# A transformer block on one core: state of the first head group taken one period later, two input chunks on a second DMA queue, startup statistics shared by ScalarE and VectorE

## The chip, the core and the metric

The kernel runs on one core of a Trainium2 chip. A time is device microseconds (us) of one execution. Each quoted time is the median of some executions, with their number and extremes where these matter. The profile of an execution counts from its first to its last instruction; this span is 2.0 to 2.15 us shorter than the time in every run of this study.

Engine names in the profile: PE is TensorE's matmul, PEld its weight load, DVE is VectorE, ACT is ScalarE, POOL is GpSimd, SP is SyncE. SPq and ACTq are DMA issues on the queues of SyncE and ScalarE. Tile names: xch is a chunk of x as loaded, lno the chunk with its mean taken off, xnT its transpose, diag the diagonal matrices of 1/std, e the probabilities, ps any PSUM buffer, and junk the unused output of a ScalarE pass that only sums.

## The reference

One block with a segment-recurrent attention and a gated MLP. What matters here is the attention with its memory (shapes: x is 2048 x 1024, 32 heads of 32, four segments of 512 tokens):

```python
x = A_x
h = x + _A_ref(_layernorm(x), A_wq, A_wk, A_wv, A_wo, A_beta)      # attention with memory
h2 = h + _B_ref(_layernorm(h), B_w_in, B_w_sp, B_b_sp, B_w_out)    # gated MLP
# in _A_ref, for each segment s:
#   p = softmax(q k^T * scale + mask); a_dot = p v
#   o = g * (phi(q) M) / (phi(q) z) + (1 - g) * a_dot
#   M = M + phi(k)^T v ;  z = z + sum phi(k)                       # the "state"
```

The state of a segment is read first in the next segment.

## The kernel before

The kernel records its operations engine by engine; the order of the program text is the order on each engine, and the waits follow from the data. Tokens are worked on in chunks of 128 (x0 to x3 are the four chunks of the first segment), heads in eight groups of four, so a segment has eight periods. The parts that the change touches:

```python
# loads at the start, all issued by SyncE: x0, x1, wv piece, x2, wv piece, x3, wv, wv, wk, ...
for k in range(8):
    if k in (0, 1, 3, 5):
        x_load((k + 1) // 2)
    else:
        i = {2: 0, 4: 2, 6: 4, 7: 6}[k]
        sp.dma_start(WV[0][:, i:i + 2, :], ...)
sp.dma_start(WK[:, :, 0:256], ...)
# ... cut ...
# startup of segment 0: mean of each chunk, centred chunk transposed on PE, 1/std applied later
warm(9)                                            # nine matmuls on dummy data
act_mean(1)                                        # ScalarE: sum of chunk 1
var0(ln_stats(XCH[0]))                             # VectorE: two statistics and their aggregate
c0 = center(0, MV[0][:, 0:1], ALU.subtract)
c1 = center(1, MEAN[1][:])
pe_Th(0, c0, dve, dve)                             # transposes of chunk 0, copies by VectorE
pe_Th(1, c1, act, dve)
# ... cut: chunks 2 and 3, v projections ...
diag(0); ... diag(3)                               # 1/std of the chunks as diagonal matrices (VectorE)
for i in range(2):                                 # and broadcast to all partitions by matmul
    pe.matmul(bank(br), ONES[:], DIAG[i][:]..., start=(i == 0), stop=(i == 1))
# ... cut ...
sp.dma_start(WK[:, :, 256:D], wcols(A_wk, 256, D))   # 1.5 MB
sp.dma_start(WQ[:, :, 256:D], wcols(A_wq, 256, D))   # 1.5 MB
phi_exp(0)
phi_max(0)                                         # ends with the DMA transpose pk <- pqk
```

In period n PE works on the logits of group n and on pv of group n-1, followed by the state of group n-1, which needs pk, a DMA transpose of phi(k):

```python
def pv(n, cqs=range(4)):
    ...                                            # probabilities times v
    if 3 in cqs:
        state(n)                                   # four matmuls ps <- v,pk
        norm(n)                                    # VectorE; calls state_sum(n): PSUM -> msum, then GpSimd
```

The softmax here doesn't subtract the row's maximum and nothing guards it: scores larger than these inputs give would overflow.

Of the kernel before, what the change touches and what calls it, by code (L numbers as in the profile page):

```python
# [6 lines left out]
F32 = mybir.dt.float32  # L7
I32 = mybir.dt.int32
ACTF = mybir.ActivationFunctionType
ALU = mybir.AluOpType  # L10

T = 2048
D = 1024
# [6 lines left out]
NQ = 8  # L20
# [237 lines left out]
def bass_sequential_preLN__memory_aug_infini_attn__mixer_gmlp__prompt_kernel(  # L258
# [14 lines left out]
    x2d = A_x[0]  # L273
    out2d = out[0]
    R = _Recorder(nc)
    pe, act, dve, pool, sp = R.pe, R.act, R.dve, R.pool, R.sp
# [6 lines left out]
    def tens(name, shape, dt, off):  # L283
        sz = int(np.prod(shape[1:])) * mybir.dt.size(dt)
        assert off % 32 == 0 and off + sz <= ARENA, (name, off, sz)
        t = nc.alloc_sbuf_tensor_at(name, list(shape), dt, offset=abase + off)
        R.space[t[:].tensor.name] = ("sbuf", off)
        return t
# [13 lines left out]
    cb = Bump(0, 14 * K)  # L302
# [5 lines left out]
    BLK = cb("blk", [128, 4], F32)  # L308
    dead = cb.c
    MASKG = cb("maskg", [128, NQ, 4, 33], F32)  # L310
    MSUM = cb("msum", [128, NQ, 132], F32)
    MZB = cb("mzb", [128, NQ, 48], BF16)
    UPD = [cb("upd%d" % i, [128, 132], F32) for i in range(2)]
    DGM = cb("dgm", [128, 4, 33], F32)
    HALF2 = cb("half2", [128, 2, 33], F32)
    MHALF = cb("mhalf", [128, 1], F32)
    STATS = [cb("stats%d" % i, [128, 2, 6], F32) for i in range(4)]
    MV = [cb("mv%d" % i, [128, 2], F32) for i in range(4)]
# [9 lines left out]
    WV = [tens("wv%d" % i, [128, 8, 512], BF16, (46 + 8 * i) * K) for i in range(2)]  # L328
# [3 lines left out]
    b1 = Bump(110 * K, 134 * K)  # L332
# [5 lines left out]
    b1 = Bump(110 * K, 120 * K)  # L338
    ONES = b1("ones", [128, 128], BF16)
    MEAN = [b1("mean%d" % i, [128, 1], F32) for i in range(4)]  # L340
    RB = b1("rb", [128, L], F32)
    DIAG = [b1("diag%d" % i, [128, 4, 128], BF16) for i in range(2)]
    JUNK = b1("junk", [128, D], BF16)
    b2 = Bump(134 * K, ARENA)
    ZSTG = [tens("zstg%d" % i, [128, 448], F32, (134 + 2 * i) * K) for i in range(4)]
    XCH = [b2("xch%d" % i, [128, D], BF16) for i in range(4)]
# [3 lines left out]
    PK = [b2("pk%d" % i, [128, 4, 128], BF16) for i in range(3)]  # L350
# [3 lines left out]
    V = b2("v", [128, 4, H, 34], BF16)  # L354
# [17 lines left out]
    PS = nc.alloc_psum_tensor("ps", [128, 8, 512], F32)  # L372
    R.space[PS[:, 0, :].tensor.name] = ("psum", 0)

    def bank(b):
        return PS[:, b, :]

    PVX = PS[:, 4:6, :].rearrange("p b w -> p (b w)")[:, 0:688].rearrange("p (q w) -> p q w", w=172)
    PVA = PVX[:, :, 0:132].rearrange("p q (i w) -> p q i w", w=33)
    STB = PS[:, 5, 176:308]  # L380

    rot = {"banks": list(range(8)), "n": 0}

# [7 lines left out]
            pe.matmul(dst, lhs(i), rhs(i), start=(i == 0), stop=(i == n - 1))  # L391


    def x_load(tc):
        sp.dma_start(XCH[tc % 4][:], x2d[tc * 128:(tc + 1) * 128, :])

    def wcols(ap, lo, hi):
        return ap[:, lo:hi].rearrange("(c p) n -> p c n", p=128)

    for k in range(8):  # L400
        if k in (0, 1, 3, 5):
            x_load((k + 1) // 2)
        else:
            i = {2: 0, 4: 2, 6: 4, 7: 6}[k]
            sp.dma_start(WV[0][:, i:i + 2, :],
                         A_wv[i * 128:(i + 2) * 128, 0:512].rearrange("(c p) n -> p c n", p=128))
    sp.dma_start(WK[:, :, 0:256], wcols(A_wk, 0, 256))
    sp.dma_start(BETAB[:], A_beta.partition_broadcast(128))
    sp.dma_start(WQ[:, :, 0:256], wcols(A_wq, 0, 256))
# [3 lines left out]
    pool.memset(MHALF[:], -0.5)  # L413
    dve.memset(ETMP[:], 0.0)
    act.activation(RDM[:, 0, 0:1], MHALF[:], ACTF.Exp)
    pool.iota(IOT[:], [[1, 128]], base=0, channel_multiplier=-1)
    pool.memset(V[:, :, :, 32:34], 1.0)
    pool.memset(BLK[:], 1.0)
# [23 lines left out]
    def ln_stats(src):  # L442
        k = lnc[0] % 4
        lnc[0] += 1
        for i in range(2):
            dve.bn_stats(STATS[k][:, i, :], src[:, i * 512:(i + 1) * 512])
        dve.bn_aggr(MV[k][:], STATS[k][:])
        return k
# [13 lines left out]
    def to_T(dst, tcl, src):  # L462
        sp.dma_start_transpose(dst[:, :, tcl * 128:(tcl + 1) * 128], src[:])
# [24 lines left out]
    def v_mm(s, tcl, half, b, i):  # L488
        pe.matmul(bank(b), XNT[s % 2][:, i, tcl * 128:(tcl + 1) * 128], WV[half][:, i, :],
                  start=(i == 0), stop=(i == 7))  # L490
# [15 lines left out]
    def qk_out(n, which, b):  # L506
        if n < NQ:
            dve.tensor_tensor(QK[n % 2][:, which, :], bank(b), RB[:], ALU.mult)
        else:
# [50 lines left out]
    def pv(n, cqs=range(4)):  # L560
        c = n % NQ
        for cq in cqs:
            for j in range(cq + 1):
                rnd, o = {0: (0, cq * 128), 1: (1, cq * 128 - 128), 2: (2, cq * 128 - 256), 3: (1, 384)}[j]
                for i in range(4):
                    pe.matmul(PVA[:, cq, i, :], E[n % 2][rnd][:, i, o:o + 128], V[:, j, 4 * c + i, 0:33],
                              start=(cq % 3 == 0 and j == 0 and i == 0), stop=False, skip_group_check=True)
        if 3 in cqs:
            state(n)
            norm(n)  # L570

    def mem(n):
# [14 lines left out]
    def norm(n):  # L587
        s, c = divmod(n, NQ)
        ot = OTOK[s % 2][:, :, c * 128:(c + 1) * 128].rearrange("p q (i d) -> p q i d", d=32)
        dve.reciprocal(RD[:], PVA[:, :, :, 32])  # L590
        dve.tensor_tensor(RD[:], RD[:], OMG[:, c:c + 1, :].to_broadcast([128, 4, 4]), ALU.mult)
        rb = RD[:].unsqueeze(3).to_broadcast([128, 4, 4, 32])
        if s == 0:
            dve.tensor_tensor(ot, PVA[:, :, :, 0:32], rb, ALU.mult)
        else:
            dve.tensor_tensor(TA[:], PVA[:, :, :, 0:32], rb, ALU.mult)
        state_sum(n)
        if s > 0:
            dve.tensor_tensor(ot, TA[:], TM[n % 2][:], ALU.add)
        if c == NQ - 1:  # L600
            for tcl in range(4):
                to_T(OT, tcl, OTOK[s % 2][:, tcl, :])

    def state(n):
        s, c = divmod(n, NQ)
        for tcl in range(4 if s < NSEG - 1 else 0):
            pe.matmul(STB, PK[n % 3][:, tcl, :], V[:, tcl, 4 * c:4 * c + 4, 0:33], start=(tcl == 0), stop=(tcl == 3))

    def state_sum(n):
        s, c = divmod(n, NQ)  # L610
        if s == NSEG - 1:
            return
        if s == 0:
            dve.tensor_copy(MSUM[:, c, :], STB)
        else:
            dve.tensor_copy(UPD[n % 2][:], STB)
            pool.tensor_tensor(MSUM[:, c, :], MSUM[:, c, :], UPD[n % 2][:], ALU.add)
        pool.tensor_tensor(DGM[:], MSUM[:, c, :].rearrange("p (i d) -> p i d", d=33), MASKG[:, c, :, :], ALU.mult)
        pool.tensor_tensor(HALF2[:], DGM[:, 0:2, :], DGM[:, 2:4, :], ALU.add)
        pool.tensor_tensor(MZB[:, c, 0:33], HALF2[:, 0, :], HALF2[:, 1, :], ALU.add)  # L620

# [34 lines left out]
    def warm(k):  # L656
        for _ in range(k):
            pe.matmul(bank(7), IDENT[:], ETMP[:, 0, :], start=True, stop=True)

    def center(tc, mean, op=ALU.add):  # L660
        o = LNO[tc % 3]
        dve.tensor_single_scalar(o[:], XCH[tc][:], mean, op)
        return o

    def act_mean(tc):
        act.activation(JUNK[:], XCH[tc][:], ACTF.Copy, scale=-1.0 / D, accum_out=MEAN[tc][:])

    def act_var(tc):
        act.activation(JUNK[:], XCH[tc][:], ACTF.Square, bias=MEAN[tc][:], accum_out=RS[tc][:, 1:2])
        pool.tensor_scalar(RS[tc][:, 0:1], RS[tc][:, 1:2], 1.0 / D, float(LN_EPS), ALU.mult, ALU.add)  # L670

    def var0(k):
        pool.tensor_single_scalar(RS[k][:, 0:1], MV[k][:, 1:2], float(LN_EPS), ALU.add)

    def rstd0(tc):
        pool.tensor_tensor(RS0[tc][:], RS[tc][:, 0:1], MHALF[:], ALU.pow)

    def diag(tc):
        dve.tensor_single_scalar(DIAG[0][:, tc, :], IDENT[:], RS0[tc][:], ALU.mult)
        dve.scalar_tensor_tensor(DIAG[1][:, tc, :], IDENT[:], RS0[tc][:], DIAG[0][:, tc, :], ALU.mult, ALU.subtract)  # L680

    def pe_Th(tcl, src, e0, e1):
        pe_T(XNT[0], tcl, src, (e0, e1))

    warm(9)
    act_mean(1)
    var0(ln_stats(XCH[0]))
    c0 = center(0, MV[0][:, 0:1], ALU.subtract)
    c1 = center(1, MEAN[1][:])
    pe_Th(0, c0, dve, dve)  # L690
    pe_Th(1, c1, act, dve)
    act_mean(2)
    rstd0(0)
    var0(ln_stats(XCH[1]))
    rstd0(1)
    c2 = center(2, MEAN[2][:])
    act_mean(3)
    vb = [next_bank() for _ in range(2)]
    for i in range(4):
        for t in range(2):  # L700
            v_mm(0, t, 0, vb[t], i)
    pe_Th(2, c2, act, dve)
    c3 = center(3, MEAN[3][:])
    for i in range(4, 8):
        for t in range(2):
            v_mm(0, t, 0, vb[t], i)
    var0(ln_stats(XCH[2]))
    rstd0(2)
    pe_Th(3, c3, act, dve)
    act_var(3)  # L710
    rstd0(3)
    diag(0)
    v_out(0, 0, 0, vb[0])
    diag(1)
# [8 lines left out]
    for i in range(2):  # L723
        pe.matmul(bank(br), ONES[:], DIAG[i][:].rearrange("p c n -> p (c n)"), start=(i == 0), stop=(i == 1))
    act.activation(RB[:], bank(br), ACTF.Copy)
    qk_out(0, 1, bk)
# [48 lines left out]
    for n in range(LAST + 1):  # L775
        s, c = divmod(n, NQ)
# [116 lines left out]
    for tb in range(4):  # L893
# [9 lines left out]
        for tcl in range(4):  # L903
            tc = 4 * tb + tcl
# [38 lines left out]
```

## Time and profile before

The time before was 796.97 us (three executions, 796.62 to 797.53). The profiled execution took 797.42 us.

The first two parts of the profile page say that TensorE is busy almost all the time (busy us, share of the span, instructions):

```profile
span 795.4 us, 13019 instructions
## 1 busy us (share of the span) xinstructions
PE 784.7 (99%) x5565; PEld 378.3 (48%) x5657; DVE 380.0 (48%) x745; ACT 295.6 (37%) x347; POOL 173.8 (22%) x329
```

The waits view for PE of the kernel before gives its idle time by cause (us in total, times, longest us); the whole execution has only six such entries, 3.6 us together, and they all lie in the first 31 us:

```profile
PE ps L209 <- DVE ident L209: 1.7, 1, 1.7
PE ps L209 <- DMA pk<-pqk: 0.8, 1, 0.8
PE ps L209 <- DVE lno L209: 0.5, 2, 0.3
...
```

The timeline of the kernel before shows the startup (start, us, engine, operation, output <- inputs, count, and in brackets the idle time before with what ended it):

```profile
3.70 1.42 DVE L209 BATCH_NORM_STATS2 stats<-xch 128x6 f32<-128x512 bf16 x2 [2.01 <-DMA xch<-in_A_x_dram]
4.31 1.06 ACT L209 ACTIVATE junk<-xch 128x1024 bf16<-128x1024 bf16 x1 [2.02 <-DMA xch<-in_A_x_dram]
5.94 1.07 PE L209 MATMUL ps<-ident,lno 128*128 128x128 bf16 x16 [0.17 <-DVE lno L209]
...
15.18 0.35 DVE L209 SCALAR_TENSOR_TENSOR diag<-ident,rs,diag 128x128 bf16<-128x128 bf16 x1
...
15.53 0.59 PE L209 MATMUL ps<-diag,ones 128*128 128x512 bf16 x2
...
19.51 0.40 PE L209 MATMUL ps<-qk 32*128 32x512 bf16 x4
```

Read it thus: x0 has landed at 3.7 us and x1 at 4.3, PE transposes from 5.94, the last diagonal is ready at 15.53 just as PE arrives, and the first logits come at 19.51. "First logits" is the mark of the startup.

The PE timeline of the kernel before, further on, shows the other wait, and the two marks between which group 1 and group 2 run:

```profile
26.11 0.40 PE L209 MATMUL ps<-qk 32*128 32x512 bf16 x4
...
29.19 0.57 PE L209 MATMUL ps<-v,e 128*128 128x33 bf16 x16
30.52 0.41 PE L209 MATMUL ps<-v,pk 128*128 128x132 bf16 x4 [0.76 <-DMA pk<-pqk]
...
34.64 0.39 PE L209 MATMUL ps<-qk 32*128 32x512 bf16 x4
...
42.25 0.39 PE L209 MATMUL ps<-qk 32*128 32x512 bf16 x4
```

The state matmuls (`ps<-v,pk`) of group 0 wait for pk. The first logits of group 1 stand at 26.11, so group 1's period takes 8.53 us, group 2's 7.61, and every later one 7.60. The chain of waits says where pk was: issued at 19.55, and 10.92 us until it landed, with 3 MB of wk and wq ahead of it in the queue.

```profile
19.55 10.92 DMA pk<-pqk
```

### The profile page before, as it was taken

The numbers are of one execution on the slowest core, as the hardware profiler recorded it, in microseconds if no ns is written. First come the engines' busy times: TensorE is split into PE (matmuls) and PEld (weight loads), VectorE is DVE, ScalarE is ACT, GpSimd is POOL, SyncE is SP. The second block draws the span as 40 slices with busy tenths as digits, with TensorE's granted clock in tenths as the row PEclk, the third lists the DMA queues.
The fourth block names the chain that finished last, engine by engine and source line by source line (L and its number), as shares of the span: only waits on it lengthen the run. The fifth ranks groups of instructions, "written<-read, shape, count | busy, mean of one in ns | idle before, by whom it ended". The sixth has DMA issues, their size and how long they took to land.

```text
span 795.4 us, 13019 instructions
## 1 busy us (share of the span) xinstructions
PE 784.7 (99%) x5565; PEld 378.3 (48%) x5657; DVE 380.0 (48%) x745; ACT 295.6 (37%) x347; POOL 173.8 (22%) x329
## 2 busy tenths in 40 slices
PE   8999999999999999999999999999999999999998
PEld 3445455554554455455544444444444444444444
DVE  7664689679954765744562000053234323323332
ACT  5777877887787675133333333100000000000000
POOL 4554565566553331100230000000000000000000
DMA  9762555353415425411116000640270143021003
GB/s 296 175 160 60 94 81 121 87 103 84 110 22 126 114 65 136 125 47 54 54 54 132 1 1 0 220 92 7 79 133 1 33 108 78 1 59 54 1 7 86
DMA packets 125002, 64.83 MB, mean 82 GB/s; under 512 B 94992, under 2 KB 113936, under 8 KB 124944
## 3 DMA queue, kind: packets, MB, share of 16 engines
q1 hardware_dynamic: 124944, 63.99, 33.7%
q8 instruction: 44, 0.72, 0.4%
q14 instruction: 14, 0.11, 0.1%
HBM read 32.51 MB, written 8.39 MB: 51 GB/s over the span
## 4 chain that ended last, share of the span: by engine, by line
PE 94%; DVE 3%; DMA 2%; issue 1%
PE ps L209 94%; DMA pk<-pqk 1%; DVE stats L209 1%; DMA xch<-in_A_x_dram 0%; DVE hch L209 0%; DVE otok L209 0%; DVE lno L209 0%; DVE pqk L209 0%; DVE ta L209 0%; DVE xnT L209 0%; DVE rd L209 0%; DVE mv L209 0%; DVE etmp L209 0%; DVE rdm L209 0%; DVE upd L209 0%
## 5 line engine op out<-in xcount | busy, mean ns | idle before, releaser
L209 PE MATMUL ps<-wspT,z 128*128 128x512 bf16 x878 | 193.1, 379 | 0.9
L209 ACT ACTIVATE e<-ps 128x2048 bf16<-128x2048 f32 (+1 forms) x96 | 152.7, 1590 | 42.4 <-PE ps L209 42.3
L209 PEld LDWEIGHTS ps<-wspT,z 128*128 128x128 bf16 x896 | 87.7, 98 | 105.7
L209 DVE TENSOR_TENSOR tmpg<-ps,brow 128x512 f32<-128x512 f32 x56 | 38.7, 691 | 196.7 <-DMA brow<-in_B_b_sp_dram 103.7
L209 POOL TENSOR_SCALAR_AFFINE_SELECT e<-e 128x512 bf16<-128x512 bf16 x128 | 90.3, 717 | 126.2 <-ACT e L209 125.9
L209 PE MATMUL ps<-win,hnT 128*128 128x448 bf16 x512 | 98.4, 352 | 0.0
L209 PE MATMUL ps<-w_out,yT 128*128 128x512 bf16 (+2 forms) x453 | 96.9, 372 | 0.5
L209 PE MATMUL ps<-hnT,win 128*128 128x512 bf16 x439 | 96.2, 379 | 0.5
L209 PEld LDWEIGHTS ps<-win,hnT 128*128 128x128 bf16 x512 | 49.7, 98 | 46.4 <-issue 0.2
L209 PEld LDWEIGHTS ps<-w_out,yT 128*128 128x128 bf16 x462 | 44.7, 98 | 52.3
L209 PEld LDWEIGHTS ps<-hnT,win 128*128 128x128 bf16 x448 | 43.8, 98 | 52.8
L209 PE MATMUL ps<-xnT,wk 128*128 128x512 bf16 x234 | 59.6, 380 | 1.2
L209 PE MATMUL ps<-wv,xnT 128*128 128x512 bf16 x255 | 59.2, 380 | 0.3 <-ACT xnT L209 0.2
L209 ACT ACTIVATE z<-ps 128x448 bf16<-128x448 f32 x60 | 32.5, 543 | 69.4 <-PE ps L209 69.4
L209 PE MATMUL ps<-wo,oT 128*128 128x512 bf16 x254 | 57.7, 379 | 0.1
L209 ACT ACTIVATE z1T<-ps 128x512 bf16<-128x512 f32 x56 | 33.4, 597 | 63.3 <-PE ps L209 63.3
L209 DVE TENSOR_TENSOR fin<-fin,ps 128x512 bf16<-128x512 bf16 (+2 forms) x33 | 22.2, 671 | 71.3 <-DMA fin<-out_dram 39.9
L209 PE MATMUL ps<-xnT,wq 128*128 128x512 bf16 x225 | 53.9, 379 | 1.8 <-issue 0.2
L209 DVE BATCH_NORM_STATS2 zst<-z 128x6 f32<-128x448 bf16 x64 | 38.9, 620 | 30.1 <-ACT z L209 30.1
L209 PEld LDWEIGHTS ps<-v,e 128*128 128x128 bf16 x1280 | 38.8, 96 | 14.0 <-issue 6.5
L209 PE MATMUL ps<-v,e 128*128 128x33 bf16 x1280 | 42.2, 178 | 0.0
L209 DVE TENSOR_TENSOR yT<-tmpg,z1T 128x512 bf16<-128x512 f32 x56 | 38.8, 692 | 1.9
(86 smaller groups left out, 611.8 us busy)
## 6 DMA issues: line engine op xcount, KB each, us to landing
xch<-in_A_x_dram SPq DMA_DIRECT2D x16, 256.0 KB, 3.5
xr<-in_A_x_dram SPq DMA_DIRECT2D x16, 256.0 KB, 4.0
out_dram<-hch SPq DMA_DIRECT2D x16, 256.0 KB, 2.4
fin<-out_dram SPq DMA_DIRECT2D x16, 256.0 KB, 2.8
out_dram<-fin SPq DMA_DIRECT2D x31, 128.0 KB, 1.7
win<-in_B_w_in_dram SPq DMA_DIRECT2D x4, 896.0 KB, 5.1
w_out<-in_B_w_out_dram SPq DMA_DIRECT2D x1, 3584.0 KB, 12.8
win<-in_B_w_in_dram SPq DMA_DIRECT2D x3, 1024.0 KB, 5.1
```

The lines of the kernel that those rows point to most:

```text
L209: ins = getattr(e, op.name)(*op.args, **op.kw)
```

## The change

Its intent is to take waits out of the start. The state of group 0 is computed one period later, with that of group 1, when pk has surely landed; x2 and x3 come through ScalarE's own DMA queue, so SyncE issues the rest sooner; chunk 0's mean is summed half by ScalarE and half by VectorE; and the variance of chunk 2 joins that of chunk 3 on ScalarE. Cut to its core:

```diff
-    STB = PS[:, 5, 176:308]
+    STB = [PS[:, 5, o:o + 132] for o in (176, 308)]
@@ loads
-    for k in range(8):  ...  (x0, x1, wv, x2, wv, x3, wv, wv on SyncE)
+    x_load(0)
+    x_load(1)
+    for i in range(0, 8, 2):
+        sp.dma_start(WV[0][:, i:i + 2, :], ...)
@@
     act.activation(RDM[:, 0, 0:1], MHALF[:], ACTF.Exp)
+    x_load(2, act)
+    x_load(3, act)
@@ pv
-            state(n)
+            if n:
+                state(n)
+            if n == 1:
+                state(0)
             norm(n)
@@ norm
-        state_sum(n)
+        if n:
+            state_sum(n)
+        if n == 1:
+            state_sum(0)
@@ startup
+    def act_half(tc):     # ScalarE: -mean of columns 0..511
+        act.activation(JUNK[:, 0:512], XCH[tc][:, 0:512], ACTF.Copy, scale=-1.0 / D, accum_out=MEAN[tc][:])
+    def dve_half(tc):     # VectorE: sum of columns 512..1023, added to it
+        dve.tensor_reduce(out=HSUM[:], in_=XCH[tc][:, 512:D], axis=mybir.AxisListType.X, op=ALU.add)
+        dve.scalar_tensor_tensor(MEAN[tc][:], HSUM[:], -1.0 / D, MEAN[tc][:], ALU.mult, ALU.add)
     warm(9)
+    act_half(0)
+    dve_half(0)
     act_mean(1)
-    var0(ln_stats(XCH[0]))
-    c0 = center(0, MV[0][:, 0:1], ALU.subtract)
+    c0 = center(0, MEAN[0][:])
+    stats0(0, 0)
     c1 = center(1, MEAN[1][:])
-    pe_Th(0, c0, dve, dve)
-    pe_Th(1, c1, act, dve)
+    pe_Th(0, c0, dve, act)
+    pe_Th(1, c1, dve, dve)
@@ ... cut ...
-    var0(ln_stats(XCH[2]))
+    act_var(2)
+    act_var(3)
+    stats0(1, 1)
+    aggr0(1)              # VectorE aggregate, then GpSimd: variance + eps, power -1/2
     rstd0(2)              # GpSimd: power -1/2
-    pe_Th(3, c3, act, dve)
-    act_var(3)
     rstd0(3)
+    pe_Th(3, c3, dve, dve)
     diag(0)
```

More of the change, by code (lines that the diff above doesn't have):

```diff
@@ L310, in bass_sequential_preLN__memory_aug_infini_attn__mixer_gmlp__prompt_kernel @@
     MASKG = cb("maskg", [128, NQ, 4, 33], F32)
-    MSUM = cb("msum", [128, NQ, 132], F32)
+    MSUM = cb("msum", [128, NQ, 136], F32)
     MZB = cb("mzb", [128, NQ, 48], BF16)
@@ L340, in bass_sequential_preLN__memory_aug_infini_attn__mixer_gmlp__prompt_kernel @@
     MEAN = [b1("mean%d" % i, [128, 1], F32) for i in range(4)]
+    HSUM = b1("hsum", [128, 1], F32)
     RB = b1("rb", [128, L], F32)
@@ L391, in mm8, with x_load @@
             pe.matmul(dst, lhs(i), rhs(i), start=(i == 0), stop=(i == n - 1))
-    def x_load(tc):
-        sp.dma_start(XCH[tc % 4][:], x2d[tc * 128:(tc + 1) * 128, :])
+    def x_load(tc, eng=sp):
+        eng.dma_start(XCH[tc % 4][:], x2d[tc * 128:(tc + 1) * 128, :])
     def wcols(ap, lo, hi):
         return ap[:, lo:hi].rearrange("(c p) n -> p c n", p=128)
-    for k in range(8):
-        if k in (0, 1, 3, 5):
-            x_load((k + 1) // 2)
-        else:
-            i = {2: 0, 4: 2, 6: 4, 7: 6}[k]
-            sp.dma_start(WV[0][:, i:i + 2, :],
-                         A_wv[i * 128:(i + 2) * 128, 0:512].rearrange("(c p) n -> p c n", p=128))
+    x_load(0)
+    x_load(1)
+    for i in range(0, 8, 2):
+        sp.dma_start(WV[0][:, i:i + 2, :], A_wv[i * 128:(i + 2) * 128, 0:512].rearrange("(c p) n -> p c n", p=128))
     sp.dma_start(WK[:, :, 0:256], wcols(A_wk, 0, 256))
@@ L606, in state @@
         for tcl in range(4 if s < NSEG - 1 else 0):
-            pe.matmul(STB, PK[n % 3][:, tcl, :], V[:, tcl, 4 * c:4 * c + 4, 0:33], start=(tcl == 0), stop=(tcl == 3))
+            pe.matmul(STB[n == 0], PK[n % 3][:, tcl, :], V[:, tcl, 4 * c:4 * c + 4, 0:33], start=(tcl == 0), stop=(tcl == 3))
     def state_sum(n):
@@ L613, in state_sum @@
         if s == 0:
-            dve.tensor_copy(MSUM[:, c, :], STB)
+            dve.tensor_copy(MSUM[:, c, 0:132], STB[n == 0])
         else:
-            dve.tensor_copy(UPD[n % 2][:], STB)
-            pool.tensor_tensor(MSUM[:, c, :], MSUM[:, c, :], UPD[n % 2][:], ALU.add)
-        pool.tensor_tensor(DGM[:], MSUM[:, c, :].rearrange("p (i d) -> p i d", d=33), MASKG[:, c, :, :], ALU.mult)
+            dve.tensor_copy(UPD[n % 2][:], STB[0])
+            pool.tensor_tensor(MSUM[:, c, 0:132], MSUM[:, c, 0:132], UPD[n % 2][:], ALU.add)
+        pool.tensor_tensor(DGM[:], MSUM[:, c, 0:132].rearrange("p (i d) -> p i d", d=33), MASKG[:, c, :, :], ALU.mult)
         pool.tensor_tensor(HALF2[:], DGM[:, 0:2, :], DGM[:, 2:4, :], ALU.add)
@@ L683, in pe_Th, with stats0, aggr0 @@
         pe_T(XNT[0], tcl, src, (e0, e1))
+    def act_half(tc):
[3 more added lines that the diff above has]
+        dve.scalar_tensor_tensor(MEAN[tc][:], HSUM[:], -1.0 / D, MEAN[tc][:], ALU.mult, ALU.add)
+    def stats0(k, i):
+        dve.bn_stats(STATS[k][:, i, :], XCH[k][:, i * 512:(i + 1) * 512])
+    def aggr0(k):
+        dve.bn_aggr(MV[k][:], STATS[k][:])
+        var0(k)
+        rstd0(k)
     warm(9)
+    act_half(0)
+    dve_half(0)
     act_mean(1)
-    var0(ln_stats(XCH[0]))
-    c0 = center(0, MV[0][:, 0:1], ALU.subtract)
+    c0 = center(0, MEAN[0][:])
+    stats0(0, 0)
     c1 = center(1, MEAN[1][:])
-    pe_Th(0, c0, dve, dve)
-    pe_Th(1, c1, act, dve)
+    pe_Th(0, c0, dve, act)
+    pe_Th(1, c1, dve, dve)
     act_mean(2)
-    rstd0(0)
-    var0(ln_stats(XCH[1]))
-    rstd0(1)
+    stats0(0, 1)
+    aggr0(0)
     c2 = center(2, MEAN[2][:])
@@ L701, in bass_sequential_preLN__memory_aug_infini_attn__mixer_gmlp__prompt_kernel @@
             v_mm(0, t, 0, vb[t], i)
-    pe_Th(2, c2, act, dve)
+    pe_Th(2, c2, dve, act)
     c3 = center(3, MEAN[3][:])
+    stats0(1, 0)
     for i in range(4, 8):
```

## The prediction

> **What bounds the kernel now.** TensorE. Part 1 of the profile page has PE busy 784.7 of 795.4 us; the chain of waits puts 94% of the span on PE. The waits view, for PE alone, adds up to 3.6 us, all in the first 31 us: 1.7 us for the identity at the start, 0.8 us for the first transpose of pk, about 1 us in pieces of 0.2 to 0.3 us. The change can only gain inside that sum, plus what it saves before the first real matmul. From 34 us the timeline shows a group every 7.60 us with no PE wait.
>
> **State of group 0 one period later (the certain part).** PE finishes pv of group 0 at about 29.6 us and starts the four state matmuls only at 30.52, when pk lands (10.9 us after its issue at 19.55, behind 3 MB of wk and wq). In the next group the step takes 0.42 us, here 1.33: 0.91 us go. The four matmuls (0.45 us) only move. The next deadline is the second wq load: it lands at 29.2 us and would be wanted at about 29.6, so it should just not bind. What comes back: in the period with both states DVE does one more copy (0.28 us, about 0.20 after overlap) before the qk copy that ended at 42.10 us, with logits at 42.25: almost no slack. I expect logits of group 3 to wait 0.1 to 0.25 us.
>
> **Startup.** Chunk 0's mean by halves replaces two statistics and an aggregate (1.67 us after landing at 3.68) by about 1.0 us, estimated from half of the 1.06 us ScalarE pass, a reduce near the 0.69 us of a 512-wide statistic, and a 0.2 us combine. But PE is in order and nine warm matmuls, one each 0.43 us, occupy it to about 5.6: first transposes at 5.6 instead of 5.94. Chunk 1's stay near 6.3, but its copies end 0.4 us earlier; chunk 2 transposes at about 8.9 (9.45 before), chunk 3 at 11.1 (11.63). Of loads on a second queue the Trainium skill, "DMA: Bandwidth & Descriptors", section "Issuing engines are not separate DMA queues", says that they run on the same 16 engines and save only issue time. I expect no more total bandwidth: DMA share is near or over 1 from 5 to 28 us.
>
> That half microsecond is mostly lost at the broadcast of the diagonals: ScalarE now runs two variances in a row (1.13 us each) to about 12.4, and GpSimd's in-order queue puts three powers (about 0.64 us each) behind the last. diag 3 ends near 15.4 to 15.8 us (15.53 before), while PE arrives at about 14.9 and waits 0.4 to 0.8 us. First logits at about 19.4 (19.51 before): startup gains 0.0 to 0.3 us.
>
> **Sum.** 0.91 + 0.15 - 0.2 = about 0.85 us. Time 796.1 us; 8 in 10 between 795.3 and 797.0. Faster by over 2%: 0.003; within 2%: 0.994; slower: 0.003.
>
> **What shows each step.** No PE wait for pk; eight state matmuls together after pv of group 1; a new PE wait for diag near 15 us; a small wait for qk before logits of group 3; group 1's period near 7.2 us, group 2's near 8.2. First transposes directly after the warm matmuls. The rest the same, shifted.
>
> **What would make it wrong.** The second wq load landing later, so that PE waits near 29.5 (gain about 0.4); wv pieces delayed by x2 and x3; powers on GpSimd overlapped, so that the startup gain reaches PE in full (gain 1.4).

## The result, and the profile after

The kernel after took 797.39 us (six executions, 797.32 to 797.70), the kernel before in the same rounds 796.79 us (six executions, 796.33 to 797.53). The ratio is 1.0008 with a 95% interval from 0.9995 to 1.0021. The time is the same within the noise, 0.6 us longer by the medians, where 0.85 us less was forecast: outside the forecast's range.

The page of the kernel after looks the same as before; a change of half a microsecond in 795 can't be read from shares. (PE's busy time is higher because fewer matmul records are missing from this trace: 5657 of 5657, against 5565 before.)

```profile
span 795.3 us, 13119 instructions
## 1 busy us (share of the span) xinstructions
PE 790.2 (99%) x5657; PEld 378.5 (48%) x5657; DVE 379.2 (48%) x745; ACT 297.1 (37%) x350; POOL 171.8 (22%) x329
```

The waits view for PE of the kernel after has no wait for pk any more, and a new one for the diagonals:

```profile
PE ps L209 <- DVE ident L209: 1.7, 1, 1.7
PE ps L209 <- DVE lno L209: 0.6, 1, 0.6
PE ps L209 <- DVE diag L209: 0.2, 1, 0.2
...
```

The timeline of the kernel after, at the start:

```profile
0.93 0.86 ACTq L209 DMA_DIRECT2D xch<-in_A_x_dram  x2
...
2.08 0.20 ACT L209 ACTIVATE rdm<-mhalf 128x1 f32<-128x1 f32 x1
...
4.07 0.69 DVE L209 TENSOR_REDUCE hsum<-xch 128x1 f32<-128x512 bf16 x1 [2.39 <-DMA xch<-in_A_x_dram]
...
5.46 1.06 ACT L209 ACTIVATE junk<-xch 128x1024 bf16<-128x1024 bf16 x1 [0.67 <-DMA xch<-in_A_x_dram]
...
5.65 0.98 PE L209 MATMUL ps<-ident,lno 128*128 128x128 bf16 x8
...
7.19 0.62 PE L209 MATMUL ps<-ident,lno 128*128 128x128 bf16 x8 [0.55 <-DVE lno L209]
...
16.04 0.35 DVE L209 SCALAR_TENSOR_TENSOR diag<-ident,rs,diag 128x128 bf16<-128x128 bf16 x1
16.06 0.10 PEld L209 LDWEIGHTS ps<-diag,ones 128*128 128x128 bf16 x1 [0.68 <-DVE diag L209]
...
20.22 0.39 PE L209 MATMUL ps<-qk 32*128 32x512 bf16 x4
```

ScalarE's two loads are issued at 0.93 us, in the midst of SyncE's first two (0.80 and 1.25), although in the program they stand behind an activation that ran at 2.08. x0 is now read from 4.07 instead of 3.70, and x1 from 5.46 instead of 4.31. (A landing in this document is the start of the first reader, where that reader waited for it.) Chunk 0 is transposed from 5.65, directly behind the warm matmuls, as forecast; but chunk 1 only from 7.19, and everything behind it is late. The first logits come at 20.22 instead of 19.51: the startup lost 0.71 us. Most of that shows only at the diagonals: wk starts at 13.98, 0.17 us later than before (13.81), and wq at 16.68, 0.72 us later (15.96). The experiments separate the two: the late loads cost about 0.7 us, the shared statistics win 0.5 us up to wk and lose it again at the diagonals.

The DMA view of the kernel after, from 3 to 5 us, has a second queue (packets, MB, share of the 16 engines). q1 is SyncE's queue; q10 is ScalarE's, since it appears only in runs with loads on ScalarE:

```profile
q10 hardware_dynamic: 225, 0.42, 54.1%
q1 hardware_dynamic: 212, 0.37, 48.3%
```

In these 2 us the second queue moved 0.42 MB and SyncE's, which carries x0 and x1, 0.37 MB; in the kernel before SyncE's queue moved 0.62 MB in the same window.

The PE timeline of the kernel after, further on, has the marks of groups 1 and 2 and the eight state matmuls between them:

```profile
26.82 0.40 PE L209 MATMUL ps<-qk 32*128 32x512 bf16 x4
...
34.19 0.39 PE L209 MATMUL ps<-qk 32*128 32x512 bf16 x4
...
37.68 0.63 PE L209 MATMUL ps<-v,pk 128*128 128x132 bf16 x8
...
42.13 0.39 PE L209 MATMUL ps<-qk 32*128 32x512 bf16 x4
```

With the first logits of group 1 at 26.82, group 1 takes 7.37 us (8.53 before) and group 2 takes 7.94 (7.61): 0.83 us are won over the two. So this pair of traces reads 0.71 lost and 0.83 won, and the spans are 0.1 us apart. That the medians are 0.6 us apart the other way is not in these two traces.

### The profile page after: what moved, and what is told of

The parts are those of the page before. It is cut to its first block, busy times and chain, and to the rows that moved or that the text cites. A ratio compares the mean times of both kernels' runs of the same rounds, so it can differ in the third digit from the quotient of the medians.

```text
span 795.3 us, 13119 instructions
## 1 busy us (share of the span) xinstructions
PE 790.2 (99%) x5657; PEld 378.5 (48%) x5657; DVE 379.2 (48%) x745; ACT 297.1 (37%) x350; POOL 171.8 (22%) x329
## 4 chain that ended last, share of the span: by engine, by line
PE 98%; ACT 1%; DMA 1%; DVE 0%; issue 0%; POOL 0%; SPq 0%; ACTq 0%
PE ps L209 98%; DMA xch<-in_A_x_dram 1%; ACT junk L209 0%; ACT e L209 0%; DVE diag L209 0%; POOL rs L209 0%; ACT xnT L209 0%; DVE lno L209 0%; DVE xnT L209 0%; SPq L209 0%; DVE fin L209 0%; ACTq L208 0%
## 5 line engine op out<-in xcount | busy, mean ns | idle before, releaser
L209 PE MATMUL ps<-xnT,wq 128*128 128x512 bf16 x256 | 60.6, 379 | 0.0
```

The lines of the kernel that those rows point to most:

```text
L209: ins = getattr(e, op.name)(*op.args, **op.kw)
```

## The experiments

Twelve kernels ran, in three lots on one chip each. The runs of the kernel before in a lot serve as its reference: medians 796.94 (lot 1), 796.89 (lot 2) and 796.49 (lot 3), nine executions each. All results were correct. The 95% intervals of the ratios to before are about 0.0013 to either side, 1 us; only that of act_late excludes 1 (1.0026, from 1.0013 to 1.0039). So what follows rests on the traces and on ranges that do not overlap. One trace per run was kept, and identical startups differ: in the five traces that share the startup of before, the first logits stand between 19.26 and 19.61.

| run | lot | median us (five executions) | lowest to highest | first logits in the trace, us |
|---|---|---|---|---|
| before_again | 1 | 797.10 | 796.60 to 798.03 | 19.61 |
| state_only | 1 | 796.62 | 796.52 to 796.79 | 19.43 |
| loads_sp | 1 | 796.66 | 796.35 to 796.85 | 19.54 |
| loads_act | 1 | 797.37 | 797.16 to 797.40 | 20.17 |
| act_late | 2 | 798.95 | 798.81 to 799.41 | 21.75 |
| pow_first | 2 | 796.35 | 796.21 to 796.73 | 19.05 |
| pow_sum4 | 2 | 796.20 | 795.96 to 796.33 | 18.82 |
| pk_ahead | 2 | 797.00 | 796.25 to 797.36 | 19.26 |
| pk_split | 3 | 796.37 | 796.34 to 796.55 | 19.47 |
| pow_sum4_split | 3 | 796.12 | 795.74 to 796.18 | 18.73 |
| pow_pk_split | 3 | 795.85 | 795.75 to 796.30 | 18.79 |
| x3_act | 3 | 796.96 | 796.93 to 797.12 | 19.82 |

### The kernel before, once more

No edit.

> The kernel before, unchanged. It asks two things. First, how much of a time lies outside the span: the kernel after had a span 0.1 us shorter than the one profile of before, and yet a median 0.6 us longer. Theory A (the one profiled execution of before, 797.42 us, was a slow one of its kind): times minus spans are 2.0 to 2.1 us for both kernels, and the spans of before spread from 794.3 to 795.5 with a median near 794.8. Rival B (a second DMA queue costs a fixed time outside the span): spans of before stay near 795.4 and times minus spans come out near 1.4 us. Second, whether the 0.91 us that PE waits for pk is the same in another execution: A expects a shorter wait in faster executions.

Times minus spans are 2.0 to 2.1 us for the kernel before, as for the kernel after and for every variant with the second queue, so rival B is out. The profiled execution of this run took 796.60 us (span 794.5), 0.8 less than the one profiled first. Its PE timeline:

```profile
29.29 0.57 PE L209 MATMUL ps<-v,e 128*128 128x33 bf16 x16
29.70 0.40 PE L209 MATMUL ps<-v,pk 128*128 128x132 bf16 x4
```

The state matmuls follow pv at once: there is no wait for pk at all. pk was issued at 19.7 and took 8.9 us, against 10.9 in the first profile. The wait that the change was sized on is one draw of something that varies; the 14 executions of before and of this copy in lot 1 spread from 796.43 to 798.03.

### The state alone

```diff
 (kernel before, with only the edits of STB, MSUM, pv, norm, state and state_sum shown above)
```

> Only the state of group 0 moves. If the prediction's first part holds by itself: no PE wait for pk, the period of group 1 about 1.1 us shorter and of group 2 about 0.3 us longer, first logits at 19.5 as before, so 0.6 to 0.9 us less than before. If the wait in typical executions of before is shorter than in the profiled one, less: 0.2 to 0.5 us.

The median is 0.32 us under that of before in the same lot, at the lower expectation. What it does is shown by the spread: 0.27 us, against 1.24 us for before (nine executions). The slow executions are gone, but the fastest of before (796.43) is faster than the fastest of this one (796.52). The trace shows why: group 1 takes 7.37 us and group 2 takes 7.95, together 15.32, while the undisturbed execution of before needs 15.21. Without a wait to remove, moving the state costs 0.1 us.

### All loads on SyncE, the rest of the change kept

```diff
 (kernel after)
-    x_load(2, act)
-    x_load(3, act)
 (and the load loop of the kernel before in place of the new one)
```

> The kernel after, with all four chunks of x loaded by SyncE in the order of before. Theory (the second queue's loads of x2 and x3 share the engines with x0 and x1, whose landing came at 4.07 and 5.46 instead of 3.68 and 4.29, and that pushed the whole startup): x1 lands near 4.3, chunk 1 transposes near 6.3 instead of 7.19, diagonals ready near 15.6 instead of 16.4, first logits at 19.3 to 19.6 instead of 20.22, time 0.6 to 0.9 us below the kernel after. Rival (the two variances in a row and the three powers behind them delay the diagonals whatever the loads do): first logits stay at 20.0 or later, time within 0.3 us of the kernel after.

796.66 us, 0.73 us under the kernel after (797.39, measured in other rounds). The timeline of this variant:

```profile
3.56 0.69 DVE L209 TENSOR_REDUCE hsum<-xch 128x1 f32<-128x512 bf16 x1 [2.02 <-DMA xch<-in_A_x_dram]
...
4.31 1.06 ACT L209 ACTIVATE junk<-xch 128x1024 bf16<-128x1024 bf16 x1
```

x0 is there at 3.56 and x1 by 4.31, and the first logits come at 19.54, not 20.22. So the loads are what made the startup late; the slowest of these five executions (796.85) is faster than the fastest of the kernel after (797.32), and than the fastest of loads_act in the same lot (797.16). But the rest of the startup change brings nothing either: this variant is level with the state alone (796.66 and 796.62 in the same lot). Its PE timeline shows the reason, which had been forecast:

```profile
13.30 1.89 PE L209 MATMUL ps<-xnT,wk 128*128 128x512 bf16 x8
15.38 0.78 PE L209 MATMUL ps<-diag,ones 128*128 128x512 bf16 x2 [0.19 <-DVE diag L209]
15.99 1.89 PE L209 MATMUL ps<-xnT,wq 128*128 128x512 bf16 x8
```

PE comes to the diagonals half a microsecond earlier than before (wk starts at 13.30, not 13.81), and then waits for them: wq starts at 15.99, against 15.96 before. The last diagonal is ready at 15.71, inside the 15.4 to 15.8 of the prediction.

### The loads alone

```diff
 (kernel before)
-    (load loop)
+    x_load(0); x_load(1); four wv pieces        # SyncE
     act.activation(RDM[:, 0, 0:1], MHALF[:], ACTF.Exp)
+    x_load(2, act)
+    x_load(3, act)
```

> The kernel before, with only x2 and x3 moved to ScalarE's queue. Theory: x1 lands near 5.4 and x0 near 4.1, first logits 0.3 to 0.7 us later than before. As pk lands behind the same loads, the wait for pk shrinks by as much as the startup grows unless pk moves too, so the end is 0 to 0.4 us later. Rival B of the first run (fixed cost of a second queue outside the span): time minus span grows by 0.5 us or more over that of before.

x0 lands at 4.05, x1 at 5.32, the first logits come at 20.17, 0.6 to 0.7 us later than in the two traces of before; the median is 0.43 us above that of before in the lot. As expected, part of the loss is hidden, since the state would often have waited for pk anyway: this trace has no wait for pk, and the spread is down to 0.24 us. Times minus spans stay at 2.05 to 2.10 us, which is a second answer against a fixed cost of the queue.

### One chunk on the second queue instead of two

```diff
 (loads_sp)
+    if k == 5: continue                         # x3 not on SyncE
     act.activation(RDM[:, 0, 0:1], MHALF[:], ACTF.Exp)
+    x_load(3, act)
```

> The variant with all loads on SyncE (796.66), with x3 alone on ScalarE's queue from its start. Half the dose. Theory (x1 lands late by the bytes that the second queue has in flight before it): x0 lands about 0.4 us late and x1 about 0.5 us late (4.7 to 4.9), first logits 0.2 to 0.5 us later than 19.54, time 796.8 to 797.1. Rival (a second queue has a cost whatever it carries): x1 as late as with both chunks, 5.4, and time near 797.4.

The ScalarE timeline of this variant, where the first pass reads x0 and the second x1:

```profile
0.93 0.38 ACTq L209 DMA_DIRECT2D xch<-in_A_x_dram  x1
...
3.70 0.63 ACT L209 ACTIVATE junk<-xch 128x512 bf16<-128x512 bf16 x1 [1.42 <-DMA xch<-in_A_x_dram]
...
5.05 1.06 ACT L209 ACTIVATE junk<-xch 128x1024 bf16<-128x1024 bf16 x1 [0.62 <-DMA xch<-in_A_x_dram]
```

x1 lands at 5.05: with none, one and two chunks on the second queue it is there by 4.31, 5.05 and 5.46 us, and the first logits come at 19.54, 19.82 and 20.22. The landing with none varies from trace to trace, but stays below the other two: the latest is 4.58, in pow_first. The landing of x1 was somewhat later and that of x0 earlier than expected, the first logits and the time (796.96) are inside. So the cost grows with what the second queue has in flight ahead of x1.

### The second queue's loads issued late

```diff
 (kernel after)
     act.activation(RDM[:, 0, 0:1], MHALF[:], ACTF.Exp)
-    x_load(2, act)
-    x_load(3, act)
@@
     act_half(0)
+    x_load(2, act)
+    x_load(3, act)
```

> The kernel after, with the two loads on ScalarE's queue issued behind its wait for x0 (about 3.6 us) instead of at 0.93 us. Theory (what cost 0.7 us was that x2 and x3 were in flight together with x0 and x1): x0 lands at 3.6 to 3.7 and x1 near 4.3 again, first logits at 19.4 to 19.7, time within 0.2 us of the variant with all loads on SyncE (796.66), though the same queue is used. Rival (loads on a second queue are costly by themselves, by slower landing or by ScalarE's issue time): x2 and x3 land so late, or ScalarE is held up so much, that first logits stay at 20 us or later and the time near 797.4.

Half of the expectation held. The ScalarE timeline of this variant:

```profile
3.45 0.63 ACT L209 ACTIVATE junk<-xch 128x512 bf16<-128x512 bf16 x1 [1.17 <-DMA xch<-in_A_x_dram]
3.46 0.86 ACTq L209 DMA_DIRECT2D xch<-in_A_x_dram  x2
...
9.19 1.06 ACT L209 ACTIVATE junk<-xch 128x1024 bf16<-128x1024 bf16 x1 [2.24 <-DMA xch<-in_A_x_dram]
```

And its PE timeline, at the transposes of chunk 2:

```profile
10.92 0.62 PE L209 MATMUL ps<-ident,lno 128*128 128x128 bf16 x8 [2.16 <-DVE lno L209]
```

x0 and x1 land early again (3.45, and x1 is read from 4.43), so the loads of x2 and x3 had indeed held them up. But x2, issued at 3.46, lands only at 9.2: 5.7 us for 256 KB. The DMA view says where the time went: up to 6.5 us no packet of the second queue moved, while SyncE's queue moved 0.83 MB from 3.46 us on; from 6.5 to 9.2 us the two moved 0.42 and 0.47 MB. Why the first packets came 3 us after the issue, where in the kernel after they came 2 us after it, is not shown. The second queue is not slower for such a load, though: in the kernel before, x3, issued on SyncE at 3.17, landed at 8.76, 5.6 us later as well. PE waits 2.16 us for chunk 2, and the time is 2.1 us above before. My expectation that x2 would still come in time was wrong: these loads are late when issued late, and make others late when issued early.

### The powers ahead of the last variance

```diff
 (loads_sp)
     act_var(2)
-    act_var(3)
+    rstd0(2)
     stats0(1, 1)
     aggr0(1)
-    rstd0(2)
+    act_var(3)
     rstd0(3)
```

> The variant with all loads on SyncE, and on GpSimd the powers of chunks 2 and 1 ahead of the work that waits for ScalarE's second variance. Theory (PE loses about 0.5 us at the diagonals, because three powers, 1.66 us, stand behind the last variance): last diagonal near 15.0 us instead of 15.7, wq at 15.5 instead of 15.99, first logits at 19.0 to 19.15 instead of 19.54, time 0.4 to 0.5 us below that variant, about 796.2. Rival (something else sets the first logits, such as rb or the wq weights): first logits stay within 0.15 us of 19.54.

In the kernel after, GpSimd's queue holds, behind the variance of chunk 3, the three powers. The GpSimd timeline of the kernel after:

```profile
13.36 0.31 POOL L209 TENSOR_SCALAR rs<-rs 128x1 f32<-128x1 f32 x1 [1.08 <-ACT junk L209]
13.73 0.22 POOL L209 TENSOR_SCALAR rs<-mv 128x1 f32<-128x1 f32 x1
14.04 1.66 POOL L209 TENSOR_TENSOR rs<-rs,mhalf 128x1 f32<-128x1 f32 x3
```

In the variant only one power is left behind it, the diagonals are done at 15.11, and PE does not wait for them. Its PE timeline:

```profile
15.07 0.59 PE L209 MATMUL ps<-diag,ones 128*128 128x512 bf16 x2
...
19.05 0.39 PE L209 MATMUL ps<-qk 32*128 32x512 bf16 x4
```

The first logits come at 19.05, as expected and 0.49 us earlier than in loads_sp. The time, 796.35, is 0.31 us under that of loads_sp by the medians (in another lot) where 0.4 to 0.5 was expected. Since startups differ from trace to trace, the stretch from the start of wk to that of wq is the better measure: it takes 2.69 to 2.70 us in after, loads_sp and x3_act, which have the shared statistics and the old order on GpSimd, and 2.15 to 2.16 us in the four variants with the powers first and in the kernel before. So the order on GpSimd was what kept the shared statistics from paying.

### The sum of group 0 where VectorE has time

```diff
 (pow_first)
-        if n == 1:
+        if n == 4:
             state_sum(0)
```

> As the run before it, and the sum of group 0's state is taken on DVE and GpSimd in the period of group 5, where DVE has no statistics of x behind it; its matmuls stay. Theory (the extra copy in the period with both states makes logits of group 3 wait 0.1 us): the period of group 2 is 0.1 us shorter, 7.83 us instead of 7.94, and the time 0.1 us lower, about 796.1. Rival: no such wait, no difference over 0.05 us.

Group 2 takes 7.84 us (32.90 to 40.74) instead of 7.95 in pow_first, so the extra copy did cost 0.1 us of PE. But in this trace group 1 takes 7.48 us instead of 7.37 (wq starts 0.1 us later in it), and the two groups together take 15.32 us as in pow_first: what was won at the copy was lost just ahead of it. The time is 0.15 us lower, 796.20; that this comes from the copy is not shown, since the first logits of the two traces already differ by 0.23 us. Three of its five executions are faster than the fastest of the nine of before in the lot (796.28).

### pk ahead of wq in the queue

```diff
 (kernel before)
-    sp.dma_start(WQ[:, :, 256:D], wcols(A_wq, 256, D))
     phi_exp(0)
     phi_max(0)
+    sp.dma_start(WQ[:, :, 256:D], wcols(A_wq, 256, D))
```

> The kernel before, with only the second wq load issued behind the first transpose of pk instead of ahead of it. Theory (the wait for pk, which differs from one execution to the next, is the queue's: pk lands only after the 3 MB ahead of it): pk lands near 25 to 26 us instead of 28.5 to 30.5, no execution waits for it, and the spread of the times, 1.6 us for before, falls below 0.5 us, with the median at 796.5 or below. The second wq load then lands near 29.7 us and may bind at 30.1. Rival (the spread comes from the landing of x, whatever pk does): the spread stays above 1 us.

pk now lands 5.4 us after its issue and nothing waits for it; but the spread is still 1.11 us and the median that of before. The waits view for PEld (from 15 to 43 us) of this variant has a new entry:

```profile
PEld ps L209 <- DMA wq<-in_A_wq_dram: 0.3, 1, 0.3
```

The wq columns of group 2 are the next deadline, half a microsecond behind that of pk, and the load had been moved behind pk. By itself this run did not decide between the theory and the rival.

### pk ahead, with the loads cut

```diff
 (kernel before)
-    sp.dma_start(WK[:, :, 256:D], wcols(A_wk, 256, D))
-    sp.dma_start(WQ[:, :, 256:D], wcols(A_wq, 256, D))
+    sp.dma_start(WK[:, :, 256:512], wcols(A_wk, 256, 512))
+    sp.dma_start(WQ[:, :, 256:512], wcols(A_wq, 256, 512))
     phi_exp(0)
     phi_max(0)
+    sp.dma_start(WK[:, :, 512:D], wcols(A_wk, 512, D))
+    sp.dma_start(WQ[:, :, 512:D], wcols(A_wq, 512, D))
```

> The kernel before, with the second wk and wq loads cut in two (columns 256 to 511 first) and the first transpose of pk issued between the halves: neither pk nor the wq columns of group 2 stand behind 3 MB any more. Theory (the spread of before is the landing of that queue against two deadlines near 29.6 us, pk and then wq, so that moving pk alone only handed the wait to wq, as the run before it had it at 0.3 us): no wait for pk or wq, spread at most 0.5 us, median 796.4 to 796.6. Rival (the spread comes from the landing of x at the start): spread of 1 us or more and waits that differ before 20 us.

The PE timeline of this variant:

```profile
29.56 0.40 PE L209 MATMUL ps<-v,pk 128*128 128x132 bf16 x4
```

This decided between the two. pk lands 4.5 us after its issue, nothing waits for pk or wq, and the spread is 0.21 us at a median of 796.37, while the state is still where it was before. Any five of the nine executions of before in this lot spread over 0.24 us or more, all nine over 0.84. So most of the spread of the kernel before comes from the queue behind which pk lands. Reordering that queue removes the wait without moving the state and without the 0.1 us of the move.

### The parts together

```diff
 pow_sum4_split: pow_sum4, wk and wq cut as above, all four loads ahead of pk
 pow_pk_split:   startup of pow_first, wk and wq cut with pk between the halves, state of group 0 not moved
```

> The best variant so far (all loads on SyncE, powers first, group 0's sum in the period of group 5) with the same cut of the loads, pk behind all of them. Theory: the 0.1 us that its PE still spends before wq of group 2 goes, median 796.0 to 796.1, spread at most 0.4 us. Rival: nothing left there, 796.2.

> The statistics of the kernel after, loads on SyncE, powers first, the cut loads with pk between them, and the state of group 0 where it was before. Theory (with pk out of the queue's way the move of the state has no work left to do): the same as the run before it within 0.15 us, 795.95 to 796.2. Rival (the move is worth something by itself): 0.3 us or more slower than that run.

Both forecasts were narrowly missed: the first has a median of 796.12 (796.0 to 796.1) and a spread of 0.44 us (at most 0.4), the second is 0.27 us faster than the first, where at most 0.15 us of difference was expected and the rival had it 0.3 us slower. The second also spreads over 0.55 us with pk out of the way, so some spread has another source, which no run isolates.

796.12 and 795.85 us, against 796.49 for before in the lot; the ratio is 0.9991 for both, with intervals up to 1.0004, though all five executions of the first (up to 796.18) are faster than all nine of before (from 796.25). In the traces groups 1 and 2 together take 15.21 us in both variants, and the first logits are 0.06 us apart: the two are the same, and the 0.27 us between the medians I leave to the noise. With pk out of the queue's way, the move of the state has nothing left to do. pow_pk_split is the simplest of the fast variants and faster than both kernels by its median.

## Why the prediction was wrong

**The bound: right.** PE's waits in the first 31 us were all there was to gain, and from 42 us on the two traces are the same, shifted by 0.1 us.

**"0.91 us go": right for the trace it was read from, too large for the kernel.** Group 1 lost its wait and became 1.16 us shorter, group 2 became 0.33 us longer (0.23 for the four matmuls that moved and, by difference, 0.10 for the new wait, forecast as 0.1 to 0.25): a net 0.83 us where 0.71 was forecast. The prediction took the four matmuls for 0.45 us (30.52 to 30.98 in the trace, where the record of the first wq matmul is missing: 7 of 8); in the kernel after the step from pk to wq takes 0.23 us per four. As the matmuls only move, this error fell out of the sum by itself: group 1 was forecast near 7.2 and came to 7.37, group 2 near 8.2 and came to 7.94. But the profile had caught a slow execution, 797.42 of 796.62 to 797.53. In another execution pk caused no wait at all, and over the medians of one lot the move is worth 0.32 us. This term was mis-sized: 0.91 stood for a median worth about 0.4 before the 0.1 us it costs (an estimate: 0.32 plus 0.1).

**"Chunk 1's stay near 6.3": the failed step.** Chunk 1's transposes started at 7.19. The prediction took the loads on the second queue to "save only issue time", so it left the landing of x1, for which these transposes wait, where it was. It gives no time for their issue; I had them in mind at about 2.3 us, behind the activation in front of them, where x0 and x1 would be almost in. They were issued at 0.93. The Trainium skill, "Perfetto Trace Analysis", section "Sequencer Loop", says that an engine's sequencer pushes engine instructions into a queue and that they wait there. I take from this that a DMA issue need not wait for the activation before it to have run. The trace agrees: 0.93 us for the issue, 2.08 for the activation. And the Trainium skill, "DMA: Bandwidth & Descriptors", section "Queues, rings and completion order", says that each DMA engine takes turns between the queue rows that have work. The runs fit this: from 3 to 5 us the two queues of the kernel after moved 0.42 and 0.37 MB, and with none, one and two chunks on the other queue, x1 is in by 4.31, 5.05 and 5.46 us. They show the shared bandwidth and its cost, not the taking of turns itself, and in act_late the second queue moved nothing for its first 3 us. I had quoted the page on saved issue time and asked what would be delayed (the wv pieces, in the last paragraph), but not the two chunks that were wanted first. The startup was forecast at +0.15 us and was -0.71; 0.73 us of the kernel's time come back when the loads go to SyncE.

**The diagonals: right.** With the loads put right, the last diagonal came at 15.71 (forecast 15.4 to 15.8) and PE lost about 0.5 us there (0.4 to 0.8), so the shared statistics gained nothing. The remedy that the prediction did not look for, another order on GpSimd, moved the first logits by 0.49 us.

**The second wq load: right** in that it just did not bind after the change; it did bind by 0.3 us when it was put behind pk.

The sum by experiment, all by medians: the state -0.32, the statistics +0.04 (loads_sp against state_only), the second queue +0.73 (the kernel after against loads_sp, other rounds), together +0.45 us; measured +0.6 us, in rounds whose noise is of the size of the difference, so that the sum comes this close is in part luck.

## What to carry to other kernels

Loads on a second queue were not free here: with two of them in flight, x1 came at 5.46 us instead of 4.31, and they were issued 1.15 us before the activation that stands ahead of them in the program. Keep what is wanted first alone, or in one queue in the order of the deadlines. Before sizing a gain on one profile, look where that execution stands among the times: here the landing behind 3 MB took 8.9 us in one and 10.9 us in another, and the spread of the times showed it. A chain shortened on one engine paid here only when the in-order queues behind it (here three powers behind the last variance) came out earlier as well.

## What the Trainium skill lacked or had wrong

- "DMA: Bandwidth & Descriptors", section "Issuing engines are not separate DMA queues", says that such DMAs interleave on the same 16 engines (the prediction took only the issue time from it), but not what the interleaving costs a load that is wanted first. Here two 256 KB loads on ScalarE's queue delayed a load on SyncE's queue from 4.31 to 5.46 us. Issued at 3.46 instead, the first of them moved no packet before 6.5 us and landed at 9.2.
- No page says plainly that a DMA written behind an activation on ScalarE is issued before that activation runs; it was, by 1.15 us (0.93 against 2.08). A wait on a semaphore, which this program writes as an instruction of its own, did hold it back (3.46, when x0 had landed at 3.45).
- No page gives the spread of landing times in a full queue: the same DMA transpose, issued at 19.6 to 19.7 us behind the same 3 MB, took 8.9 us in one execution and 10.9 us in another, and the kernel's times spread over 1.24, 1.94 and 0.84 us in the three lots of nine, 0.21 us once that queue was reordered.
- "VectorE: DVE Perf Modes", section "Rules for kernel authors", calls a reduce the slowest operation of VectorE. Here a 128x512 bf16 reduce took 0.69 us, just as a 128x512 statistic did, so it was no slower than what it replaced; no other operation was compared.
